# Attention with a feed-forward layer on one core: the last output tile copied by one engine, and the last stores merged

## The chip, the cores and the metric

The kernel runs on one core of a Trainium2 chip. The core has a matrix engine (TensorE, PE in the rows), a vector engine (VectorE, DVE), a scalar engine (ScalarE, ACT), GpSimd (POOL) and a queue engine (SyncE, SP) that only issues transfers. Sixteen DMA engines move the data of all transfers, whichever engine issues them. The metric is the device time of one execution in microseconds (us); lower is better.

## The reference

Attention over 32 global and 512 local positions, for 8 batches of 8 heads with 64 elements each: global queries see all 544 positions, local queries see the 32 global ones and a window of 32 to either side. The result, 4352 rows of 512, goes through a feed-forward layer with an exact GELU.

```
out_g = softmax(q_g @ k_all.T / 8) @ v_all
out_l = softmax([q_l @ k_g.T, masked(q_l @ k_l.T)] / 8) @ [v_g, v_l]
x     = rows of [out_g, out_l], batch after batch      # 8 * 544 rows of 512
h     = x @ w_in                                       # 512 -> 2048
out   = (0.5 * h * (1 + erf(h / sqrt(2)))) @ w_out     # 2048 -> 512, float32
```

In the output each batch owns R = 544 rows of 512 floats (2 KB a row): SG = 32 rows of global positions first, 512 of local ones behind them.

## The kernel before

The rows are worked on in 17 chunks of 256. Sixteen of them are the halves of a batch's local rows (their key is a pair of batch and half), and the seventeenth, key "g", holds the 32 global rows of all 8 batches. For each chunk the feed-forward layer's second product adds up in two accumulators of 128x512 (`acc`, one per tile t of 128 rows), by three matmuls for each of 16 blocks of the hidden layer (`ml_o`, L1359 to L1361). `graph()` lists the steps with what they need, take and free; `plan()` decodes a written-out order of all steps with the engine of each, and the loop at the end issues them in that order, each engine's instructions one behind the other.

The chunk "g" is the last one. In it the last two blocks of the hidden layer are done for tile 0 first and then for tile 1, so that tile 0 is complete six matmuls ahead of the end. Step `ob` (`ml_e`) copies an accumulator into an output tile `o` of 128 partitions by 512 floats; step `ow` (`ml_w`) stores it. For the other chunks a tile's 128 rows are one piece of the output, stored by one transfer of 256 KB from SP (L1382). For chunk "g", 32 partitions belong to each of four batches, whose 32 rows lie 544 rows apart, and the kernel issues four transfers of 64 KB for each tile (L1378): for tile 0 two from SP and two from GpSimd, for tile 1 two from SP and two from ScalarE. Tile 0 is copied whole by ScalarE; tile 1 is copied in two halves of 256 columns, the first by ScalarE, the second by VectorE.

Behind the last step, SP waits for everything that is outstanding, and the engines meet at a closing exchange (L1462).

Of the kernel before, what the change touches and what calls it, by code (L numbers as in the profile page):

```python
# [11 lines left out]
F32 = mybir.dt.float32  # L12
# [210 lines left out]
def graph():  # L223
    B, NP, NF, NCC = 8, 4, 16, 4
# [10 lines left out]
    def iss(name, n):  # L235
        if name[0] == "wl":
            return 0.45
        c = 99
        if len(name) > 1 and isinstance(name[1], tuple) and len(name[1]) == 3 and isinstance(name[1][0], int):
            c = 8 * name[1][0] + 4 * name[1][1] + name[1][2]  # L240
        if name[0] == "lv" and c < 8:
            return 0.66 * n
        if name[0] in ("lk", "lq") and c < 8:
            return (0.78 if name[0] == "lk" else 0.6 if c < 4 else 0.75) * n
        if name[0] in ("lk", "lq") and c < 14:
            return 0.6 * n
        return (0.47 if c >= 16 else 0.55) * n

    def one(y):
        return (JOINT[y[0]], y) if y[0] in JOINT else y  # L250

    def step(name, fn, args, eng, due, needs=(), takes=(), frees=(), dur=None, issues=0, size=0.0, table=None, early=False, port=True, after=None):
        takes, frees = [one(y) for y in takes], [one(y) for y in frees]
        d = DUR.get(dur or name[0], 0.0)
        eng = eng if name[1:] in (("g", NF // 2 - 1), ("g", 1)) else (EARLY if early else LATER).get(name[0], eng)
        late = len(name) > 1 and (isinstance(name[1], int) and name[0][0] != "w" or isinstance(name[1], tuple) and name[1][0] >= 2)
        nodes[name] = dict(name=name, fn=fn, args=args, due=due, needs=[x for x in needs if x is not None], after=after,
                           takes=list(takes), frees=list(frees), size=size, table=table, port=port and name[0] in PORT,
                           eng=({k: d[k] for k in eng} if isinstance(d, dict) else
                                {k: (d if not issues else iss(name, issues)) for k in eng}))  # L260
# [21 lines left out]
    for g in range(NF // 2):  # L282
        d = 290.0 + 15.0 * (g // 2) + 7.0 + 3.75 * (g % 2)
        rk = "rg"
        for j in range(2):
            n = 8 * (g // 2) + 4 * j + 2 * (g % 2)
# [12 lines left out]
    for n, u in enumerate(units):  # L299
# [39 lines left out]
        w = n < NF32  # L339
# [23 lines left out]
        g = (b, p // 2) if half else None  # L363
# [61 lines left out]
    LAG = LAGS  # L425
# [4 lines left out]
    for n, key in enumerate(keys):  # L430
        plain = n < NPL
        if plain:
            C0, W = CS[n], CW[n]
        else:
            k, bh = divmod(n - NPL, 2)
            C0, W = TS[k] + 10.0 - 3.25 * LAG - 1.0 + 52.0 * bh, 3.25
# [5 lines left out]
        for f in range(NF if plain else 0):  # L442
            hb = [("h", (key, f // 2))] if f % 2 == 0 else []
            w = [("w3", 2 * f)] if not n else [("w5", 2 * f)] if n == 1 else []
# [23 lines left out]
        for f in range(NF // 2):  # L468
            d = C0 + W * (2 * f + 2)
            if not plain:  # L470
                q, o = divmod(f, 2)
# [3 lines left out]
                at = run.index(f)  # L475
                d = C0 + W * (2 * at + 1)
# [11 lines left out]
        for t in range(2):  # L488
            step(("ob", key, t), "ml_e", (key, t), "a", C0 + W * (NF + LAG) + 1.5 + 0.1 * t,
                 [("mo", key, NF - 2 + t if key == "g" else NF - 1), ("ob", key, 0) if t and key != "g" else None], [("at%d" % (1 - t), (key, t, "o"))], [("acc", key)])  # L490
            step(("ow", key, t), "ml_w", (key, t), "s" if key == "g" else "sp", C0 + W * (NF + LAG) + 2.0 + 0.1 * t, [("ob", key, t)], [], [("at%d" % (1 - t), (key, t, "o"))], issues=4 if key == "g" else 1, size=0.26)


    for k, T in enumerate(TS):
# [14 lines left out]
        W, X, Y = ([("h", (k, q, x)) for q in range(4)] for x in "WXY")  # L509
        for n, (q, i) in enumerate(ORDER):  # L510
            Q = T + 1.5 * n if i < 3 else T + 46.0 + 13.0 * q + {6: 0.0, 5: 1.5, 7: 5.5, 3: 7.0, 4: 8.5}[i]
            more = {1: [], 2: [("sd", k, q)], 6: [("se", k, q)], 5: [], 7: [("z", k, q)], 3: [("z", k, q)], 4: [("cc", k, q)]}[i]
            w = []
            if not k:
                w = [("ya", 8 * q + x) for x in ((4, 6) if i == 4 else (0, 2))] if i in (1, 2, 4) else [("sx", 2 * q + r, FORM[i] // 5, x) for r in range(2) for x in range(2)]
# [17 lines left out]
def plan():  # L533
    wl, nodes = graph()
    names = list(nodes)
    order = []
    for v in struct.unpack("<%dH" % len(names), zlib.decompress(base64.b85decode(SEQ))):
        x = nodes[names[v // 6]]
        x["on"] = "tavps-"[v % 6]
        order.append(x)  # L540
    return wl, order
# [3 lines left out]
def attn_mlp(ctx, tc, q_l, k_l, v_l, q_g, k_g, v_g, w_in, w_out, out):  # L545
    nc = tc.nc
    B, H, S, D = q_l.shape
    SG = q_g.shape[2]
    DM = H * D
    FF = w_in.shape[1]  # L550
    P = 128
    NCC = DM // P
    NF = FF // P
    NP = H // 2
    R = SG + S
    CH = 256
# [3 lines left out]
    ap_ = ctx.enter_context(tc.tile_pool(name="ap", bufs=1))  # L560
# [16 lines left out]
    for half in range(2):  # L577
        m = (cp if half else mp).tile([P, WF], BF16, name=f"mask{half}")
        nc.gpsimd.memset(m, 0.0)
        for c0, k0, w in (((0, -32, 32), (64, 0, 160)) if half == 0 else ((0, -32, 160), (192, 128, 32))):  # L580
            v = m[:, c0:c0 + w]
# [7 lines left out]
    st = {}  # L589
# [9 lines left out]
    def copy(e, out, in_):  # L599
        if e == "a":  # L600
            nc.scalar.activation(out=out, in_=in_, func=AF.Copy)  # L601
        elif e == "v":
            nc.vector.tensor_copy(out=out, in_=in_)
        else:
            nc.gpsimd.tensor_copy(out=out, in_=in_)
# [112 lines left out]
    def by(e):  # L718
        return {"a": nc.scalar, "p": nc.gpsimd, "s": nc.sync}[e]
# [641 lines left out]
            nc.tensor.matmul(out=acc[t], lhsT=gh[:, f % 2, tsl], rhs=lo, start=False, stop=(f == NF - 1))  # L1361

    def ml_e(e, key, t):
        o = ap_.tile([P, DM], F32, name="ob", tag=f"at{1 - t}")
        acc = st[key, "acc"][t]
        st[key, "ob", t] = o
        if key == "g" and t:
            copy("a", o[:, 0:CH], acc[:, 0:CH])
            copy("v", o[:, CH:DM], acc[:, CH:DM])
        else:  # L1370
            copy(e, o, acc)

    def ml_w(e, key, t):
        o = st.pop((key, "ob", t))
        if key == "g":
            for n in range(4):
                r0 = (4 * t + n) * R
                ((nc.sync, nc.gpsimd)[n % 2] if t == 0 else (nc.sync, nc.scalar)[n % 2]).dma_start(out=out[r0:r0 + SG, :], in_=o[32 * n:32 * n + 32])  # L1378
        else:
            b, half = key  # L1380
            r0 = b * R + SG + half * CH + t * P
            by(e).dma_start(out=out[r0:r0 + P, :], in_=o)  # L1382
# [84 lines left out]
```

## Time and profile before

| what | value |
|---|---|
| time, median of 3 runs | 993.09 us (992.3 to 993.37) |
| the profiled execution's own time | 991.57 us |
| its span, first to last instruction | 989.8 us |
| TensorE busy | 971.6 us (98% of the span) |
| granted TensorE clock, mean | 0.998 of full speed |
| DMA, mean over the span | 177 GB/s |

The span is what the trace covers; the execution's own time is 1.77 us longer, and the median of the runs lies 1.52 us above that execution. Times in rows are counted from the start of the span.

### The profile page before, as it was taken

To read this page: it belongs to the slowest core of one execution; us is meant where nothing else is said; L and a number is where in the kernel's file an instruction comes from. 1 tells how busy PE (TensorE), PEld (TensorE's weight loads), DVE (VectorE), ACT (ScalarE), POOL (GpSimd) and SP (SyncE) were. 2 spreads that over 40 slices of the span, in tenths; PEclk is the share of its full clock that TensorE was granted. 3 is DMA by queue.
4 is the path that set the end of the run, shared out by engine and by line. 5 is a ranking of instruction groups with operands and counts; after the bars stand their busy time and mean duration, and the time that the engine had idled before them with its cause. 6 is when DMAs were issued, how large, how long until landed. Compare 5 with 4: busy or idle time off the path is not lost.

```text
span 989.8 us, 21297 instructions
## 1 busy us (share of the span) xinstructions
PE 971.6 (98%) x6712; PEld 860.9 (87%) x6712; DVE 728.6 (74%) x2192; ACT 719.6 (73%) x1714; POOL 432.0 (44%) x456
## 2 busy tenths in 40 slices
PE   7999999999999999999999999999999999999998
PEld 5767798998989999988989889988999899988986
DVE  5988999778889988878878987677977775323210
ACT  5888988787777777887979788668877877453331
POOL 6322757244343464345524563345533554243133
PEclk9999999999999999999999999999999999999999
DMA  9996232545536899858786778757777668646630
GB/s 225 256 264 196 57 72 54 126 113 143 130 76 157 242 280 272 257 131 205 198 222 162 186 186 253 184 140 185 200 232 182 183 182 225 201 145 222 203 108 21
DMA packets 307728, 175.05 MB, mean 177 GB/s; under 512 B 256256, under 2 KB 279040, under 8 KB 307616
## 3 DMA queue, kind: packets, MB, share of 16 engines
q1 hardware_dynamic: 304064, 171.07, 64.3%
q0 software_dynamic: 1344, 1.97, 0.8%
q8 instruction: 53, 0.87, 0.4%
q10 hardware_dynamic: 2208, 0.66, 0.3%
q14 instruction: 59, 0.48, 0.2%
HBM read 149.49 MB, written 24.12 MB: 175 GB/s over the span
## 4 chain that ended last, share of the span: by engine, by line
PE 93%; DMA 3%; DVE 1%; ACT 1%; SPq 1%; issue 0%; POOL 0%; ACTq 0%; DVEq 0%
PE hb L1313 23%; PE acc L1359 11%; PE acc L1361 11%; PE acc L1360 11%; PE o L1016 5%; PE s L905 5%; PE h L1209 3%; PE h L1210 3%; PE h L1211 3%; PE h L1205 3%; PE t L979 3%; PE acc L1351 3%; PE go L1149 2%; PE sg L1062 2%; PE o L1029 2%; PE t L980 1%
## 5 line engine op out<-in xcount | busy, mean ns | idle before, releaser
L1359 PE MATMUL acc<-wh,gh 128*128 128x512 f32 x512 | 203.3, 397 | 0.0
L1361 PE MATMUL acc<-wl,gh 128*128 128x512 f32 x512 | 200.5, 392 | 0.0
L1360 PE MATMUL acc<-wh,gl 128*128 128x512 f32 x512 | 200.3, 391 | 0.0
L608 POOL TENSOR_TENSOR gl<-gf,gh 128x512 fp32r<-128x512 f32 x80 | 107.0, 1338 | 169.5 <-ACT gh L601 21.6
L1313 PE MATMUL hb<-fh,rt 128*128 128x256 f32 x960 | 178.8, 282 | 0.7 <-DMA rt<-wd 0.7
L1313 PEld LDWEIGHTS hb<-fh,rt 128*128 128x128 f32 x960 | 150.8, 189 | 1.9 <-DMA rt<-wd 0.9
L1313 PE MATMUL hb<-fl,rt 128*128 128x256 f32 x480 | 134.1, 279 | 0.0
L778 ACT ACTIVATE a_t<-a_t,sm 128x192 f32<-128x192 f32 (+1 forms) x256 | 117.0, 459 | 15.2 <-DVE sm L930 14.4
L1361 PEld LDWEIGHTS acc<-wl,gh 128*128 128x128 f32 x512 | 96.1, 188 | 20.7
L1359 PEld LDWEIGHTS acc<-wh,gh 128*128 128x128 f32 x512 | 96.9, 189 | 16.9
L1360 PEld LDWEIGHTS acc<-wh,gl 128*128 128x128 f32 x512 | 96.4, 188 | 16.0
L608 POOL TENSOR_TENSOR vs<-vr,vs 128x512 fp32r<-128x512 f32 x56 | 73.0, 1303 | 82.8 <-ACT vs L601 17.9
L778 ACT ACT_TABLE_LOAD x71 | 91.1, 1283 | 10.4 <-PE acc L1361 2.7
L924 DVE CUSTOM_DVE_ANT_0 a_t<-s,mask 128x192 f32<-128x192 f32 (+1 forms) x256 | 81.1, 367 | 16.9 <-PE s L905 15.3
L608 POOL TENSOR_TENSOR gl<-gq,gh 128x512 fp32r<-128x512 f32 x47 | 61.0, 1301 | 68.0 <-PE acc L1361 28.2
L1313 PEld LDWEIGHTS hb<-fl,rt 128*128 128x128 f32 x480 | 90.3, 188 | 0.4
L601 ACT ACTIVATE at<-t 128x512 fp32r<-128x512 f32 (+1 forms) x112 | 59.1, 542 | 27.4 <-PE t L982 17.7
L1209 PE MATMUL h<-xh,wh 128*128 128x256 f32 x256 | 75.5, 295 | 1.0 <-ACT gf L778 1.0
L999 DVE TENSOR_TENSOR at<-t,at 128x512 fp32r<-128x512 f32 (+1 forms) x112 | 67.1, 614 | 9.7 <-ACT at L601 8.9
L1313 PE MATMUL hb<-xf,rt 128*128 128x256 f32 x576 | 72.5, 281 | 0.9 <-DVE sm L924 0.9
L1210 PE MATMUL h<-xl,wh 128*128 128x256 f32 x256 | 71.9, 281 | 0.0
L1211 PE MATMUL h<-xh,wl 128*128 128x256 f32 x256 | 71.9, 281 | 0.0
(193 smaller groups left out, 2301.2 us busy)
## 6 DMA issues: line engine op xcount, KB each, us to landing
rt<-wd SPq DMA_DIRECT2D x168, 512.0 KB, 4.5
wraw<-in_moe_w_in_dram SPq DMA_DIRECT2D x16, 512.0 KB, 5.7
wraw<-in_moe_w_out_dram SPq DMA_DIRECT2D x16, 512.0 KB, 6.7
raws<-in_v_l_dram SPq DMA_DIRECT2D x64, 128.0 KB, 3.3
out_dram<-ob SPq DMA_DIRECT2D x32, 256.0 KB, 3.2
raws<-in_k_l_dram SPq DMA_DIRECT2D x224, 36.0 KB, 2.4
raws<-in_q_l_dram SPq DMA_DIRECT2D x224, 32.0 KB, 2.8
vr<-in_v_l_dram SPq DMA_DIRECT2D x48, 128.0 KB, 4.2
```

The source lines that it names most:

```text
L601: nc.scalar.activation(out=out, in_=in_, func=AF.Copy)
L608: (nc.vector if e == "v" else nc.gpsimd).tensor_sub(**kw)
L778: nc.scalar.activation(func=func, **kw)
L924: nc.vector.tensor_tensor_reduce(out=a_t[:, j, aoff[half][i]:aoff[half][i] + w], in0=s[:, c:c + w], in1=masks[half][i], scale=1.0, scalar= ...
L999: nc.vector.tensor_sub(out=at[:, 1], in0=st.pop((u, "t", j))[:, :n * P].rearrange("p (n q) -> p n q", q=P), in1=at.bitcast(F32)[:, 0])
L1209: nc.tensor.matmul(out=h, lhsT=hi, rhs=xh, start=(c == 0 and f % 2 == 0), stop=False, skip_group_check=True)
L1210: nc.tensor.matmul(out=h, lhsT=hi, rhs=xl, start=False, stop=False, skip_group_check=True)
L1211: nc.tensor.matmul(out=h, lhsT=lo, rhs=xh, start=False, stop=(c == NCC - 1), skip_group_check=True)
L1313: nc.tensor.matmul(out=h[:, r], lhsT=a, rhs=b, start=(i in (1, 5) and r == 0 and c == 0 and n == 0), stop=(c == 1 and n == 2), skip_group_ ...
L1359: nc.tensor.matmul(out=acc[t], lhsT=gh[:, f % 2, tsl], rhs=hi, start=(f == 0), stop=False)
L1360: nc.tensor.matmul(out=acc[t], lhsT=gl[:, f % 2, tsl], rhs=hi, start=False, stop=False)
L1361: nc.tensor.matmul(out=acc[t], lhsT=gh[:, f % 2, tsl], rhs=lo, start=False, stop=(f == NF - 1))
```

## The change

The last tile of chunk "g" is copied whole by ScalarE. Tile 0's four stores become one transfer from SP, whose DRAM side is a pattern of 4 blocks of 32 rows, 544 rows apart. Tile 1's four stores become two transfers, one of two blocks (64 partitions, 128 KB) from ScalarE's queue and one of two blocks from SP's. GpSimd issues none of them any more. The number of issues in the step's description changes with it; the written-out order of the steps is the same.

```diff
-            step(("ow", key, t), "ml_w", (key, t), "s" if key == "g" else "sp", ..., issues=4 if key == "g" else 1, size=0.26)
+            step(("ow", key, t), "ml_w", (key, t), "s" if key == "g" else "sp", ..., issues=1, size=0.26)
...
     def ml_e(e, key, t):
-        o = ap_.tile([P, DM], F32, name="ob", tag=f"at{1 - t}")
         acc = st[key, "acc"][t]
-        st[key, "ob", t] = o
-        if key == "g" and t:
-            copy("a", o[:, 0:CH], acc[:, 0:CH])
-            copy("v", o[:, CH:DM], acc[:, CH:DM])
-        else:
-            copy(e, o, acc)
+        st[key, "ob", t] = o = ap_.tile([P, DM], F32, name="ob", tag=f"at{1 - t}")
+        copy(e, o, acc)

     def ml_w(e, key, t):
         o = st.pop((key, "ob", t))
         if key == "g":
-            for n in range(4):
-                r0 = (4 * t + n) * R
-                ((nc.sync, nc.gpsimd)[n % 2] if t == 0 else (nc.sync, nc.scalar)[n % 2]).dma_start(out=out[r0:r0 + SG, :], in_=o[32 * n:32 * n + 32])
+            v = out[4 * R * t:4 * R * t + 4 * R, :].rearrange("(n r) w -> n r w", r=R)[:, 0:SG, :]
+            if t:
+                nc.scalar.dma_start(out=v[0:2], in_=o[0:64])
+                nc.sync.dma_start(out=v[2:4], in_=o[64:128])
+            else:
+                nc.sync.dma_start(out=v, in_=o)
```

## Rows read from the trace of the kernel before

**Rows 1.** The page: span; busy time and share of TensorE; chain by engine.

```profile
span 989.8 us, 21297 instructions
...
PE 971.6 (98%) x6712; PEld 860.9 (87%) x6712; DVE 728.6 (74%) x2192; ACT 719.6 (73%) x1714; POOL 432.0 (44%) x456
...
PE 93%; DMA 3%; DVE 1%; ACT 1%; SPq 1%; issue 0%; POOL 0%; ACTq 0%; DVEq 0%
```

**Rows 2.** Timeline from 984.2: start, us, engine, line, what, [idle before <- releaser].

```profile
983.74 0.60 ACT L601 ACTIVATE ob<-acc 128x512 f32<-128x512 f32 x1 [8.83 <-PE acc L1361]
...
984.36 2.48 SPq L1378 DMA_DIRECT2D out_dram<-ob  x4
...
984.63 1.06 POOL L1378 DMA_DIRECT2D out_dram<-ob  x2 [5.76 <-ACT ob L601]
984.67 0.39 PE L1361 MATMUL acc<-wl,gh 128*128 128x512 f32 x1
985.10 0.38 ACT L601 ACTIVATE ob<-acc 128x256 f32<-128x256 f32 x1 [0.76 <-PE acc L1361]
985.51 0.42 DVE L603 COPY ob<-acc 128x256 f32<-128x256 f32 x1 [5.11 <-ACT ob L601]
985.97 0.94 ACTq L1378 DMA_DIRECT2D out_dram<-ob  x2
```

**Rows 3.** Chain that ended last, from 985: start, us, what.

```profile
984.83 0.24 PE acc L1361
985.07 0.02 issue
```

**Rows 4.** Timelines from 985.9 and 986.35: the last tile's stores one by one.

```profile
985.97 0.88 SPq L1378 DMA_DIRECT2D out_dram<-ob  x2
...
986.33 0.52 SPq L1378 DMA_DIRECT2D out_dram<-ob  x1
986.38 0.53 ACTq L1378 DMA_DIRECT2D out_dram<-ob  x1
```

**Rows 5.** Stores of the output, 984 to 991: issue to landing.

```profile
DMA to landing us min/median/max: 1.6/1.9/2.1
```

**Rows 6.** SP's waits from 984: in total, times, longest.

```profile
SPq L1462 <- DMA out_dram<-ob: 1.5, 1, 1.5
```

**Rows 7.** Closing instructions, 988.45 to 989.05: count, ns min/median/max, first and last start.

```profile
L1462 SPq EVENT_SEMAPHORE  x8: 28/28/28, 988.5 to 988.9; - x8
L1462 SPq DRAIN  x2: 7/7/7, 989.0 to 989.0; - x2
L1462 POOLq DRAIN  x1: 3795/3795/3795, 985.1 to 985.1; - x1
```

**Rows 8.** DMA view, 984 to 990, 40 slices of 0.15 us.

```profile
DMA  0000000088179923903989598920000000000000
GB/s 0 0 0 0 0 0 0 0 218 191 28 191 218 383 82 137 273 27 96 246 205 259 164 287 205 219 69 0 0 0 0 0 0 0 0 0 0 0 0 0
DMA packets 352, 0.52 MB, mean 87 GB/s; under 512 B 128, under 2 KB 128, under 8 KB 352
```

**Rows 9.** Stores of the output, 961 to 962: issue time and landing.

```profile
L1382 SPq DMA_DIRECT2D out_dram<-ob x2: 332/378/424, 961.1 to 961.5; - x2
...
DMA to landing us min/median/max: 2.0/2.2/2.3
```

**Rows 10.** DMA view, 961 to 964, 40 slices of 0.075 us.

```profile
GB/s 0 0 0 0 0 0 0 0 0 0 0 0 27 273 410 410 382 382 355 437 437 273 383 383 382 410 410 382 410 382 300 164 0 0 0 0 0 0 0 0
DMA packets 288, 0.52 MB, mean 175 GB/s; under 512 B 32, under 2 KB 32, under 8 KB 288
```

**Rows 11.** Stretches: us, busy of PE, PEld, DVE, ACT, POOL, PEclk, DMA share, GB/s.

```profile
962.00:963.00 1.00, 1.00 (x11) 1.00 (x10) 0.38 (x1) 1.00 (x3) 0.00 (x0) 1.00 1.01 379
...
987.00:988.00 1.00, 0.00 (x0) 0.00 (x0) 0.00 (x0) 0.00 (x0) 0.00 (x0) 1.00 0.84 209
988.00:989.00 1.00, 0.00 (x0) 0.00 (x0) 0.00 (x0) 0.00 (x0) 0.00 (x0) 0.70 0.01 2
```

More of the change, by code (lines that the diff above doesn't have):

```diff
@@ L490, in graph @@
                  [("mo", key, NF - 2 + t if key == "g" else NF - 1), ("ob", key, 0) if t and key != "g" else None], [("at%d" % (1 - t), (key, t, "o"))], [("acc", key)])
-            step(("ow", key, t), "ml_w", (key, t), "s" if key == "g" else "sp", C0 + W * (NF + LAG) + 2.0 + 0.1 * t, [("ob", key, t)], [], [("at%d" % (1 - t), (key, t, "o"))], issues=4 if key == "g" else 1, size=0.26)
+            step(("ow", key, t), "ml_w", (key, t), "s" if key == "g" else "sp", C0 + W * (NF + LAG) + 2.0 + 0.1 * t, [("ob", key, t)], [], [("at%d" % (1 - t), (key, t, "o"))], issues=1, size=0.26)
     for k, T in enumerate(TS):
```

## The prediction

> **What bounds the kernel now.** I read the page first. TensorE is busy for 98% of the span and carries 93% of the chain that ended last [rows 1], so a change in time must either touch TensorE's stream or come before its first or behind its last matmul. The edit touches neither the order of the steps nor anything issued before the copies of the last chunk, so what counts is the stretch behind the last matmul. The timeline of that stretch is next [rows 2]: the last matmul's row begins at 984.67, and the chain has TensorE's last piece end at 985.07 [rows 3]. From there nothing computes. ScalarE copies one half of the last tile (985.10, 0.38 us), VectorE the other half behind it and not beside it (985.51, 0.42 us; its idle time ended with ScalarE's copy), and four stores of 64 KB go out, two from SP at 985.97 and 986.33 and two from ScalarE at 985.97 and 986.38 [rows 2, 4]. Stores of this stretch land 1.6 to 2.1 us after their issue [rows 5]. SP's wait for them takes 1.5 us [rows 6], after which eight short waits run from 988.5 to 988.9, then a drain [rows 7], and a closing exchange between the engines to 989.8. So 4.7 us lie behind the last matmul, and the change can work on these alone.
>
> What the transfers do there is in the DMA view. All eight stores of 64 KB leave 352 packets, 128 of them under 512 B: sixteen small ones per transfer, and 224 larger ones [rows 8]. Two whole-tile stores of 256 KB, issued at 961.1 and 961.5 [rows 9], leave 288 packets, 32 under 512 B, that is again sixteen small ones each, and 256 rows of 2 KB [rows 10]. I read the sixteen as one completion mark from each of the 16 DMA engines. In every one of these transfers the DRAM side's outermost loop counts rows, 32 or 128 of them.
>
> **The change part by part.** The sum is made against the profiled execution, 991.57 us with a span of 989.8; the three runs' median, 993.09, is 1.52 above it, and I add that at the end.
>
> *The copy.* ScalarE's half copy and VectorE's copy go. In their place stands one copy of 128x512, which took 0.60 us for the tile before [rows 2]. It runs from 985.10 to 985.70, and the stores behind it go out at 985.73 in place of 985.97: 0.24 us earlier. VectorE has nothing else to do there.
>
> *The stores of the first tile.* Two SP issues and two POOL issues become one SP issue of 256 KB. A whole-tile issue took 0.33 to 0.42 us of SP's queue [rows 9], so SP is free before 984.8, long before 985.73. POOL's issues (1.06 us) go; POOL's drain ran to about 988.9, just inside SP's waits [rows 2, 7], so nothing is won or lost by it. Data began to move 0.84 us after the issue (984.36 to the slice that begins at 985.2) [rows 2, 8].
>
> *The stores of the last tile.* Two SP and two ScalarE issues become one each, of 128 KB, both at 985.73. Nothing queues behind either but the end of the program.
>
> *How the new transfers are dealt out.* This decides the case, and no transfer in the trace shows it. The DRAM side of the new stores is no longer a run of rows: the blocks of 32 rows lie 544 rows apart and can't be flattened, so the outermost loop counts 4 blocks for the first tile and 2 for each half of the last. One bound is that rows still go over all 16 DMA engines, as in [rows 8, 10]. The other is that a transfer is dealt out by its outermost loop, so that four DMA engines serve the first store and two each half of the last, all counted from the first engine on. I take the second: the division by the outermost count is the one thing that the old and new stores don't share, and 32 and 128 both divide by 16 where 4 and 2 don't. The Trainium skill says so outright (DMA: Bandwidth & Descriptors, "Why a DMA increments its semaphore by 16 and not by 1"): a transfer uses the largest number of engines, at most 16, that divides the outermost counts of both sides, and from SP and ScalarE's queues these are the lowest-numbered ones. No run here shows a count under 16; the sixteen small packets agree with it as far as they go. By that rule the sum is the one worked out now; without it, it is that of the first rival.
>
> Price of the second bound. In the window 962 to 963, filled by whole-tile stores, 16 engines moved 379 GB/s [rows 11]: 23.7 GB/s each, a row of 2,048 B in 86.5 ns. Engines 0 and 1 get 32 rows each of the first tile (128 by four), and 32 rows of each half of the last (64 by two): 96 rows, 8.30 us. They start at 985.20, and since their first 32 rows last to 987.97 while the last tile's data can start at 985.73 + 0.84 = 986.57, they don't run dry. The last row is stored at 985.20 + 8.30 = 993.50. Before, data ended by about 988.1: the second from 987 moved 209 GB/s, that from 988 only 2 [rows 11]. So the end comes 5.4 us later.
>
> *The waits at the end.* In the program, SP's last waits go through the stores' eight completion counters in a fixed order, and the transfers take the counters in turn. Before, ScalarE's last store had a counter that is asked for second, and eight waits followed, 0.06 us each (988.46 to 988.96) [rows 7]. With three transfers fewer on SP and ScalarE's queues, the last counters stand about five places further back, and the waits ahead of them pass while the data still moves: 0.3 us less.
>
> Sum: +5.4 - 0.3 = +5.1 us; the span becomes 994.9, the profiled time 996.7, and the median 998.2 us. Bounds of the rate: the best slices of the whole-tile stores moved 437 GB/s [rows 10], 75 ns a row, hence 96 rows in 7.2 us and +4.0 in all (997.1); in the window 987 to 988 the 64 KB stores moved 209 GB/s at a share of 0.84 [rows 11], 131 ns a row, hence 12.6 us and +9.4 (1002.5).
>
> **Rivals.**
> 1. *All 16 engines serve the new stores.* For it: every store of the trace has its sixteen small packets [rows 8, 10]. Against it: none of them has an outermost count below 32. Issue at 985.73, landing 2.0 to 2.3 us later as for the whole-tile pair [rows 9], so 987.7 to 988.0 where SP's wait ended at about 988.4; with the 0.3 us of waits that is 0.7 to 1.0 us less than before: 992.1 to 992.4, not to be told from no change. It decides from eight engines up: with eight for each store an engine gets 16 + 8 + 8 rows, 2.8 us, and ends at 988.0, still no later than before; with four it would end at 990.7.
> 2. *Few engines, but each store its own.* The first tile ends at 987.97; each half of the last has 32 rows per engine, 986.57 + 2.77 = 989.34: 1.2 later, less 0.3, +0.9: 994.0. Nothing in the trace speaks for or against.
> 3. *The two halves of the last tile share two engines, but the first tile uses others.* 64 rows, 5.54 us from 986.57: 992.1, +4.0 - 0.3: 996.8.
> 4. *The change is worth more than it seems,* because fewer stores also meet less contention at the end: beyond 2 us. The 64 KB stores' slower rows (131 against 86.5 ns) speak for some of it, but the whole stretch behind the last copy is only 3.9 us long, most of it latency.
>
> **How the numbers follow.** Chances: the forecast 0.74, rival 1 0.12, rival 2 0.05, rival 3 0.06, rival 4 0.03. A change of 0.2%, 2.0 us, is about what a measurement of this kernel can tell from none (its three runs lie 1.07 us apart). Slower: the forecast and rival 3, 0.80. Same: rivals 1 and 2, 0.17. Faster: rival 4, 0.03. The forecast's own range is 997 to 1002.5. The range reaches down to rival 2 and leaves out rivals 1 and 4 and the forecast's very end: 993.8 to 1002.
>
> **What would show it.** In the DMA view of the end: 8 small packets in place of 48 if four, two and two engines serve the stores, and about 47 GB/s for several microseconds, a share of two sixteenths. The copy should be one of 0.60 us, the three issues at 984.36 and 985.73, the two landings together near 8 us after issue, and few of SP's short waits behind them. Everything before 983.7 should be as it was. The prediction is wrong if the small packets number 48, or if the engines that serve the stores differ between them.

## The result, and the profile after

The changed kernel takes 1001.11 us (median of 6 runs, 998.39 to 1003.15) against 993.23 us for the kernel before. The ratio is 1.0078, with a 95% interval of 1.0062 to 1.0095: slower, by 7.9 us between the medians. A second sample on another occasion gave 1.0068 (1.0040 to 1.0095).

The profiled execution of the changed kernel took 1001.41 us, with a span of 999.4 us. The timeline behind its last matmuls, with the columns of [rows 2]:

```profile
987.19 0.68 SPq L1376 DMA_DIRECT2D out_dram<-ob  x1
...
987.50 0.39 PE L1361 MATMUL acc<-wl,gh 128*128 128x512 f32 x1
987.92 0.60 ACT L601 ACTIVATE ob<-acc 128x512 f32<-128x512 f32 x1 [0.76 <-PE acc L1361]
988.55 0.55 SPq L1374 DMA_DIRECT2D out_dram<-ob  x1
988.55 1.39 ACTq L1373 DMA_DIRECT2D out_dram<-ob  x1
```

From the start of the last copy to the end of the span the kernel before took 989.8 - 985.10 = 4.7 us [rows 1, 2]. Here it is 999.4 - 987.92 = 11.5 us, so 6.8 us are lost in that stretch. I call this length the tail; all comparisons below go by it. The DMA view of the same stretch, 984 to 999, shows why:

```profile
DMA packets 264, 0.52 MB, mean 35 GB/s; under 512 B 8, under 2 KB 8, under 8 KB 264
```

The bytes are those of [rows 8], but three stores leave 8 packets under 512 B in place of 16 for each store. Four, two and two make eight. The stretches of one microsecond, with the columns of [rows 11]:

```profile
988.00:989.00 1.00, 0.00 (x0) 0.00 (x0) 0.00 (x0) 0.52 (x1) 0.00 (x0) 1.00 0.20 25
989.00:990.00 1.00, 0.00 (x0) 0.00 (x0) 0.00 (x0) 0.00 (x0) 0.00 (x0) 1.00 0.18 10
990.00:991.00 1.00, 0.00 (x0) 0.00 (x0) 0.00 (x0) 0.00 (x0) 0.00 (x0) 0.80 0.23 63
991.00:992.00 1.00, 0.00 (x0) 0.00 (x0) 0.00 (x0) 0.00 (x0) 0.00 (x0) 0.50 0.25 98
992.00:993.00 1.00, 0.00 (x0) 0.00 (x0) 0.00 (x0) 0.00 (x0) 0.00 (x0) 0.50 0.21 80
993.00:994.00 1.00, 0.00 (x0) 0.00 (x0) 0.00 (x0) 0.00 (x0) 0.00 (x0) 0.50 0.13 49
994.00:995.00 1.00, 0.00 (x0) 0.00 (x0) 0.00 (x0) 0.00 (x0) 0.00 (x0) 0.50 0.14 53
```

The last two numbers of a row are the share of the 16 DMA engines that was busy and the GB/s. Up to 990 little moves, though the first store was issued at 987.19; I call this the stall. From 991 to 992 a quarter of them is busy, that is four, at 98 GB/s. From 993 on it is an eighth, two engines, at 49 to 53 GB/s, although both halves of the last tile have been issued since 988.55. So the two stores share the same two engines, and while the first tile's store is under way no engine beyond its four is at work: the last tile waits behind the first one. The queues say so too. SP's queue is q1 and ScalarE's is q10 (66 packets in all, 64 rows and 2 small ones), and the DMA view from 990.4 to 992.9 has q1 alone:

```profile
DMA packets 108, 0.21 MB, mean 85 GB/s; under 512 B 4, under 2 KB 4, under 8 KB 108
...
q1 hardware_dynamic: 108, 0.21, 23.4%
```

The first tile's four small packets are in it, and ScalarE's half has moved nothing yet. SP's waits, in total, times and longest, are the other side of it [rows 6]:

```profile
SPq L1460 <- DMA out_dram<-ob: 8.9, 2, 5.1
```

The rest of the difference lies ahead of the edit. In the kernel before, the stores of the other chunks began between these times:

```profile
L1382 SPq DMA_DIRECT2D out_dram<-ob x32: 332/400/1102, 134.2 to 961.5; - x32
```

and in the changed kernel, whose line for them is two lower:

```profile
L1380 SPq DMA_DIRECT2D out_dram<-ob x32: 333/401/1876, 135.9 to 964.3; - x32
```

The instructions up to there are the same in both, and 1.7 us of the delay are there before the first of these stores. The granted TensorE clock shows where these 1.7 us come from. From 10 to 14 us TensorE was busy for 2.35 us in the kernel before and 2.37 us in the changed one, at full clock; from 14 to 22 us the clock stood at the lower of its two levels (1.2 GHz in place of 2.4) for part of the time, and for longer in the changed kernel. The rows are those of the kernel before, then of the changed one, with the columns of [rows 11]:

```profile
14.00:22.00 8.00, 7.54 (x45) 5.76 (x45) 6.21 (x24) 5.14 (x17) 4.07 (x8) 0.79 1.04 269
```

```profile
14.00:22.00 8.00, 7.71 (x34) 4.99 (x33) 6.30 (x27) 6.11 (x20) 2.79 (x6) 0.57 0.97 254
```

A mean of 0.57 in place of 0.79 over 8 us is 1.8 us of full clock, about the 1.7 us. All ten profiles of this study agree: the first store begins at 132.8 to 133.7 where this stretch has a clock of 1.00, at 134.2 to 134.9 with 0.79 to 0.83, and at 135.9 and 136.0 with 0.57. It does not go with the edit, since a second profile of the changed kernel (`after_again`) is among those with 1.00. Why the clock differs between executions is open. So this pair of profiles differs by 9.6 us of span, of which only 6.8 belong to the change. 6.8 of 993.2 us is 0.68%, inside both intervals.

### The profile page after: what moved, and what is told of

Read it like the earlier page. It is cut to its first block, busy times and chain, and to the rows that moved or that the text cites. A ratio compares the mean times of both kernels' runs of the same rounds, so it can differ in the third digit from the quotient of the medians.

```text
span 999.4 us, 21290 instructions
## 1 busy us (share of the span) xinstructions
PE 975.7 (98%) x6712; PEld 862.1 (86%) x6712; DVE 727.8 (73%) x2191; ACT 720.4 (72%) x1714; POOL 432.4 (43%) x454
## 4 chain that ended last, share of the span: by engine, by line
PE 84%; DVE 5%; DMA 4%; ACT 3%; SPq 1%; issue 1%; POOL 0%; DVEq 0%; ACTq 0%; POOLq 0%
PE hb L1313 21%; PE acc L1359 10%; PE acc L1361 10%; PE acc L1360 10%; PE o L1016 5%; PE s L905 5%; PE h L1205 3%; PE acc L1351 3%; PE t L979 3%; PE h L1209 2%; PE h L1210 2%; PE h L1211 2%; PE go L1149 2%; PE sg L1062 2%; PE o L1029 2%; PE t L980 1%
```

## The experiments

Two groups of four kernels ran, each group with the kernel before on the same chip. A single microsecond is hard to see in the times, since the part ahead of the edit scatters, so each experiment is read by its tail, and by the number of small packets in it, which tells how many engines served its stores. A store that only two or four engines serve is called narrow. Tails are worked out from the times of the traces before rounding. The times are given beside them, and they bear the tails out: wherever there is a median, it differs from that of the kernel before by what the tail differs, within 1.1 us.

| kernel | tail, us | small packets | ratio to before (95%) |
|---|---|---|---|
| before | 4.7 | 128 | |
| `copy_whole` | 4.6 | 128 | 0.9989 (0.9976 to 1.0002) |
| `row_order_one` | 4.1 | 32 | 0.9987 (0.9967 to 1.0006) |
| `row_order` | 4.4 | 48 | 1.0013 (0.9999 to 1.0027) |
| `last_four` | 7.2 | 68 | 1.0018 (1.0006 to 1.0031) |
| `lone_narrow` | 7.4 | 68 | one run, 995.45 us |
| `one_last` | 9.0 | 8 | 1.0039 (1.0018 to 1.0060) |
| `first_four` | 10.6 | 68 | 1.0056 (1.0025 to 1.0088) |
| changed | 11.5 | 8 | 1.0078 (1.0062 to 1.0095) |
| `after_again` | 11.5 | 8 | 1.0068 (1.0040 to 1.0095) |

**The copy alone** (`copy_whole`, against the kernel before):

```diff
-        if key == "g" and t:
-            copy("a", o[:, 0:CH], acc[:, 0:CH])
-            copy("v", o[:, CH:DM], acc[:, CH:DM])
-        else:
-            copy(e, o, acc)
+        copy(e, o, acc)
```

> The kernel before with the last tile copied whole by ScalarE, its eight stores of 64 KB kept. Measured from the start of the copy behind the last matmul to the end of the span, 4.7 us before and 11.5 us after the change. Theory (the new stores pile up on the first DMA engines, the copy is harmless): 4.5 us, 0.24 us less than before, and a time that cannot be told from before. Rival (the whole copy delays the stores): more than 4.7 us.

Its timeline, and the line of landings for the stores of its tail:

```profile
984.03 0.60 ACT L601 ACTIVATE ob<-acc 128x512 f32<-128x512 f32 x1 [0.76 <-PE acc L1361]
984.66 0.85 ACTq L1374 DMA_DIRECT2D out_dram<-ob  x2
...
DMA to landing us min/median/max: 1.6/2.0/2.2
```

The stores go out 0.63 us behind the copy's start in place of 0.87, as expected, but land up to 2.2 us after their issue in place of 2.1 [rows 5], and the span leaves a tail of 4.6 us: of the 0.24 us less than 0.1 arrive. Why the landings take longer was not settled. Earlier ones would hardly have helped. GpSimd's closing drain, which stands ahead of its part in the closing exchange, ran from 984.0 to 987.8, and SP's last wait ended at 987.8 too:

```profile
L1458 POOLq DRAIN  x1: 3795/3795/3795, 984.0 to 984.0; - x1
```

So as long as GpSimd stores half of the first tile, the tail is hardly shorter than 4.5 us (an estimate: 3.8 us from the copy's start to the end of the drain, and 0.74 us of exchange behind it in this trace). The copy costs nothing, so the loss is in the stores.

**One tile narrow, the other not** (`last_four`, `first_four`, against the changed kernel). In the first, only the last tile's stores are four of 32 rows again:

```diff
             if t:
-                nc.scalar.dma_start(out=v[0:2], in_=o[0:64])
-                nc.sync.dma_start(out=v[2:4], in_=o[64:128])
+                for n in range(4):
+                    (nc.sync, nc.scalar)[n % 2].dma_start(out=v[n], in_=o[32 * n:32 * n + 32])
```

> The changed kernel, but the last tile goes out in four stores of 32 rows (SP and ScalarE, two each); the first tile's store keeps its pattern of four blocks. Theory (dealt out by the outermost count, from the first engine on): engines 0 to 3 get 32 rows of the first tile and 8 of the last, 40 rows of 0.08 us each; 5.3 us from the last copy's start to the end, 6.7 if the stall of 1.4 us near the first rows comes back; about 70 small packets (4 + 4 x 16 = 68). Rival (the first tile's pattern is what costs, by its slow start): 8 us or more.

In the second, only the first tile's:

```diff
             else:
-                nc.sync.dma_start(out=v, in_=o)
+                for n in range(4):
+                    (nc.sync, nc.gpsimd)[n % 2].dma_start(out=v[n], in_=o[32 * n:32 * n + 32])
```

> The changed kernel, but the first tile goes out in four stores of 32 rows as before (SP and GpSimd); the last tile keeps its two stores of two blocks. Theory: engines 0 and 1 get 64 rows of the last tile and some 8 of the first; 8.4 us from the last copy's start to the end, 9.8 with a stall of 1.4 us, and 4 + 64 = 68 small packets. If the two stores of the last tile used engines of their own: 32 rows each, about 5.9 us.

The small packets are those expected in both, 4 + 64. The tails, 7.2 and 10.6 us, are longer than expected by 0.5 and 0.8 us with the stall counted in. In `last_four` even the stores of 32 rows land late, behind the one narrow store that was issued ahead of them, and some are slow to issue:

```profile
L1374 SPq DMA_DIRECT2D out_dram<-ob x2: 353/588/822, 987.4 to 987.8; - x2
L1374 ACTq DMA_DIRECT2D out_dram<-ob x2: 386/634/882, 987.4 to 987.8; - x2
...
DMA to landing us min/median/max: 4.9/5.0/5.1
```

That is 4.9 to 5.1 us where stores of the same size took 1.6 to 2.1 [rows 5]. So a narrow store also holds up stores behind it that spread over all engines. The rival that the first tile's pattern alone makes the loss fails, since `first_four` without it is the slower of the two. That the halves of the last tile use engines of their own fails too: that would have been 5.9 us.

**Both tiles on four engines** (`one_last`, against the changed kernel):

```diff
-            if t:
-                nc.scalar.dma_start(out=v[0:2], in_=o[0:64])
-                nc.sync.dma_start(out=v[2:4], in_=o[64:128])
-            else:
-                nc.sync.dma_start(out=v, in_=o)
+            nc.sync.dma_start(out=v, in_=o)
```

> The changed kernel, but the last tile too goes out in one store of four blocks from SP, so that four engines serve both tiles. Theory (an engine's rows set the end): 64 rows on each of four engines, 5.1 us, in place of 96; 8.9 us from the last copy's start to the end, 7.5 without the stall; 8 small packets. Rival (a narrow store costs a fixed time, whatever its rows per engine): no less than 11 us.

It came out at 9.0 us, as the theory had it. The same bytes with 64 rows on the busiest engines in place of 96 end 2.5 us sooner than in the changed kernel: 0.08 us for each of the 32 rows. Beside the start and the stall, what sets the end is the number of rows on the busiest engine.

**One narrow store by itself** (`lone_narrow`): the first tile as in `first_four`, the last one as in `one_last`.

> The first tile in four stores of 32 rows as before, the last tile in one store of four blocks from SP, with no other store issued behind it. Theory: 32 rows on each of four engines behind a start of 1.29 us; 5.8 us from the last copy's start to the end if the stall comes from other stores that are issued meanwhile, 7.0 to 7.5 if a narrow store stalls by itself; 68 small packets.

The tail is 7.4 us, so the stall comes with a narrow store even when nothing is issued behind it. Its DMA view from 985.0 to 995.9, slices of 0.27 us:

```profile
GB/s 0 0 0 0 210 90 210 211 226 15 23 53 15 15 8 8 68 75 68 98 98 113 98 105 75 45 0 0 0 0 0 0 0 0 0 0 0 0 0 0
```

Behind the first tile's traffic (slices 5 to 9, up to 226 GB/s) the narrow store starts with 53 GB/s, falls to 8, and only then moves about 100 GB/s to its end.

**The changed kernel again** (`after_again`, nothing edited):

> The changed kernel once more. What lies behind the last copy's start took 11.5 us: 96 rows of 0.08 us on engines 0 and 1 are 7.7, and 1.2 us of the rest are a stall in which the first store's rows take 0.35 to 1.0 us each. If the stall belongs to the stores' pattern: 11.2 to 11.8 us again. If it was chance: about 10.2 us. What lies before the last copy (987.9 us here, 985.1 in the profile of before) should differ by a few us from profile to profile, since the instructions there are the same: theory, anything from 984 to 989.

The tail is 11.5 us once more, stall included, so the stall belongs to the stores. The last copy started at 987.44 here. Over the ten profiles of this study it started between 984.03 (`copy_whole`) and 988.97 (`row_order`). The two with the old stores, 984.03 and 985.10, are the earliest. Ten profiles alone can't rule out an effect of the edits, but the times speak for scatter: the kernel before alone took 990.18 to 998.70 us in 20 runs of one group, and the medians follow the tails.

**All 16 engines for large stores** (`row_order`, against the changed kernel). The rows of the last chunk are put into another order in the output tile, row first and batch second, so that the outermost loop on the DRAM side runs over rows. The order is made where the last GELU results are written, and costs no further instruction:

```diff
+    def rows(x):
+        return x.rearrange("p f (t r n) -> p (f t) n r", t=2, n=4)
+    def toks(x):
+        return x.rearrange("p f (t n r) -> p (f t) n r", t=2, n=4)
...
+            if key == "g" and o == 1:
+                act(AF.Gelu, out=rows(gf), in_=toks(st["hb", k, q, y]))
+                return
...
-        nc.vector.tensor_add(out=t[:, 1], in0=st["hb", k, q, "X"], in1=st["q"])
+        ro, tn = (rows, toks) if k == len(TS) - 1 else (lambda x: x, lambda x: x)
+        nc.vector.tensor_add(out=ro(t[:, 1]), in0=tn(st["hb", k, q, "X"]), in1=tn(st["q"]))
...
+            v = v.rearrange("n r w -> r n w")
             if t:
-                nc.scalar.dma_start(out=v[0:2], in_=o[0:64])
-                nc.sync.dma_start(out=v[2:4], in_=o[64:128])
+                nc.scalar.dma_start(out=v[0:16], in_=o[0:64])
+                nc.sync.dma_start(out=v[16:32], in_=o[64:128])
```

> The three stores of the changed kernel, but the last chunk's rows are put in another order in the output tile (row first, batch second), by writing the last GELU results in that order, so that the outermost loop on the DRAM side counts 32, 16 and 16 rows. Theory: all 16 engines serve each store, 48 small packets, 3.8 to 4.0 us from the last copy's start to the end, 0.7 to 1.0 us less than before; the GELU and add instructions that write in steps of four may take longer but lie beside TensorE. Rival (three large stores to rows of four batches are slow in themselves, whatever engines serve them): 8 us or more.

Same bytes, same three queues, same rows in DRAM; of the stores only the order of the loops differs. The small packets are 48 and the tail is 4.4 us in place of 11.5. This is the run that shows the cause: a large store to blocks 544 rows apart is not slow in itself. The tail is 0.4 us longer than the 3.8 to 4.0 expected; the stores land 2.4 to 2.7 us after their issue, where the whole tiles of [rows 9] took 2.0 to 2.3.

The new order is not free for the engines that make it. Behind 925 us four of ScalarE's GELUs take 1111 ns each, against 592 in the changed kernel (first line here, then the changed kernel's), and four of VectorE's additions 1075 against 692:

```profile
L778 ACT ACTIVATE gq<-hb 128x512 f32<-128x512 f32 x4 | 4.2, 1111 | 0.8 <-PE hb L1322 0.8
```

```profile
L778 ACT ACTIVATE gq<-hb 128x512 f32<-128x512 f32 x4 | 2.3, 592 | 0.8 <-PE hb L1313 0.8
```

They lie beside a busy TensorE, and the times show no loss from them: 1.0013 here and 0.9987 for the next kernel.

**The same with one store for each tile** (`row_order_one`):

```diff
...
-            if t:
-                nc.scalar.dma_start(out=v[0:2], in_=o[0:64])
-                nc.sync.dma_start(out=v[2:4], in_=o[64:128])
-            else:
-                nc.sync.dma_start(out=v, in_=o)
+            nc.sync.dma_start(out=v.rearrange("n r w -> r n w"), in_=o)
```

> The tile in row order (row first, batch second), one store for each tile, both from SP, outermost count 32. Theory: all 16 engines, 32 small packets, 4.2 to 4.6 us from the last copy's start to the end, near the 4.4 of the same order with the last tile in two stores; no stall.

Its DMA view from 987.2 to 998.1, and its issues and landings:

```profile
GB/s 0 0 0 0 0 75 413 383 90 0 165 398 376 23 0 0 0 0 0 0 0 0 0 0 0 0 0 0 0 0 0 0 0 0 0 0 0 0 0 0
DMA packets 288, 0.52 MB, mean 48 GB/s; under 512 B 32, under 2 KB 32, under 8 KB 288
```

```profile
L1382 SPq DMA_DIRECT2D out_dram<-ob x2: 574/602/629, 987.5 to 988.9; - x2
...
DMA to landing us min/median/max: 2.4/2.5/2.5
```

Each tile moves at some 400 GB/s, and the tail is 4.1 us: 0.6 us shorter than before, the shortest of all, and under the 4.5 us that GpSimd's drain would have left. The time can't tell 0.6 us from none (0.9987, 0.9967 to 1.0006). It is the version to keep, by its tail.

## Why the prediction was right

The forecast was 998.2 us with a range of 993.8 to 1002, slower; the measured 1001.11 lies in it, on the high side. There is some luck in that: the range reaches up to 1002 for a slow rate, which did not come, and this room took up a stall that the sum did not have.

*The copy.* Right: one copy of 0.60 us, and the stores 0.24 us earlier. Alone it brought less than 0.1 us.

*How the stores are dealt out.* Right, and it decides the case. The changed kernel has the 8 small packets, the shares of four and two sixteenths, and the pile-up of both halves on two of the first store's four engines; `row_order` undoes it with the order of the loops alone. The rule of the Trainium skill (DMA: Bandwidth & Descriptors, "Why a DMA increments its semaphore by 16 and not by 1") is what these traces show for counts of 4 and 2, and with 16 engines for counts of 16 and 32; which engines they are by number no view tells, only that the stores share them. Rivals 2 and 3 are out by the changed kernel's rows and by `first_four`, rival 4 by the time. Rival 1 describes what `row_order` then did, where its condition was met, though with 0.3 us less than before and not 0.7 to 1.0.

*The rate.* Right, a little high: 86.5 ns a row was forecast; 98 GB/s over four engines are 84 ns, and 51 over two are 80.

*The start.* This term was mis-sized. The sum let data move 0.84 us after the issue and then without a break. Measured, the first store was issued at 987.19 and data began in the slice from 988.45, 1.3 us later, as the DMA view from 988 to 991 (slices of 0.075 us) has it:

```profile
GB/s 0 0 0 0 0 0 82 55 55 0 109 0 27 0 0 0 0 55 27 0 0 0 0 27 0 0 55 55 55 27 82 27 55 82 82 55 55 55 82 109
```

Up to 990 the engines then moved 25 and 10 GB/s, though their busy share of 0.20 and 0.18 is not far from the later 0.25. The last rows came at about 998.0, 10.1 us after the copy's start where 8.4 was forecast. The 96 rows took 9.55 us from the first to the last; at 80 to 84 ns each they are 7.7 to 8.1, so the stall is 1.5 to 1.9 us. With 0.43 us for the later start (0.53 us behind the copy's start in place of 0.10), less what the rows were quicker (0.2 to 0.6), that makes the 1.7 us by which the end came later than forecast. The later start comes with the block pattern and not with few engines: `row_order_one` too took 0.6 us to issue, and its data began in the slice from 988.59, at least 1.1 us after the issue at 987.50, with 16 engines. The stall was seen with few engines alone: the two kernels in row order have none, `lone_narrow` has it. Its size is what is left over of the sum, and what the engines wait for in it is open.

*The waits at the end.* Right: the last wait ended at 998.4, with three short ones and the drain behind it to 998.6 in place of eight [rows 7], and 1.4 us lie between the last data and the end in place of 1.7. Only the landing came later than the 8 us after issue that were forecast: 9.8 us, by the start above.

```profile
L1460 SPq EVENT_SEMAPHORE  x3: 28/28/28, 998.4 to 998.5; - x3
L1460 SPq DRAIN  x2: 7/7/7, 998.6 to 998.6; - x2
```

So the tail grew by 6.8 us where 5.1 was forecast. The rest of the 7.9 us between the medians lies ahead of the last copy or in the scatter of the runs; the interval, 6.2 to 9.4 us, has room for both.

*"Everything before 983.7 as it was"* held for the instructions and not for the clock on the wall: that part differed by up to 4.9 us between profiles of nearly the same work, part of it by the granted clock near the start.

## What to carry to other kernels

Before merging small stores into one with a pattern, look at its outermost loop: a count of 2 or 4 left 2 or 4 of the 16 DMA engines here, and several such stores piled up on the same ones. Count the rows on the busiest engine, here 96 of 0.08 us, or read the number of small packets in the DMA view; if it is below 16 for each store, change the order of the data so that the long loop comes first. At the end of a program nothing hides such a transfer, so there the tail behind the last matmul tells more than the total time.

## What the runs showed of the hardware that I had not expected

- Issues are longer among stores that few engines serve: ScalarE's half of the last tile took 1.39 us to issue, against 0.64 us in `row_order` with 16 engines, and in `last_four` the second stores of 32 rows behind the narrow one took 0.82 and 0.88 us, against 0.52 and 0.53 before. Why is not shown.
- The first rows of such a store are slow and cost 1.5 to 1.9 us, in two profiles of the changed kernel alike; a share of 0.18 is shown as busy while 10 GB/s move.
- A store with one more loop in its pattern took 0.54 to 0.69 us of SP's queue, whatever the number of engines, against 0.33 to 0.42 for a plain tile [rows 9].
- GpSimd's closing drain took 3.8 us where GpSimd stored half of the first tile ([rows 7], `copy_whole`), and ended as late as the waits for the last stores. In the changed kernel, where it stores nothing at the end, it took 4.3 us but began at 980.4, 7.5 us ahead of the last copy.
